# Chunks of v joined three steps ahead, and a fixed order of val, x and output on TensorE in the last batch

## The chip, the cores and the metric

One Trainium2 chip, one core of it. The metric is the device time of one execution in microseconds (us); lower is better. The engines are TensorE (PE), VectorE (DVE), ScalarE (ACT), GpSimd (POOL) and SyncE (SP), which here only issues DMAs.

## The reference

Four batches of 6336 rows and 256 channels. Per batch a channel attention: the scores are 256 x 256, and v is multiplied by the softmax `a`. Then a gated causal convolution over the rows.

```python
qn = q / (norm(q, axis=1) + 1e-06)          # over the 6336 rows; k alike
s = kn.transpose(0, 2, 1) @ qn / tau
a = softmax(s)                              # 256 x 256 for each batch
x = v @ a
gate = sigmoid(sum(conv_w[k] * xp[:, k:k + S] for k in range(5)))   # xp: x with 4 rows of zeros ahead
out = (gate * (x @ w_val)) @ w_out
```

## The kernel before

For each batch the kernel first works through groups of rows of q and k (scores and squares of norms), then a softmax, then the rows of v in 13 chunks of 508 rows (the last one 240). There are 52 such chunks, called steps here, numbered 0 to 51; the last batch's are 39 to 51. The scores of a batch are made between the steps of the batch before it, so steps 40 and later have no scores beside them.

The work of one step n, by function and line:

- v arrives with channels on partitions, as a high part `v_hi` and a remainder `v_lo` (TensorE multiplies the pairs in three products). Up to step 41 and for step 51 TensorE transposes it (`transpose_v`, L486). For steps 42 to 50 (`FROM = 42`) DMAs do it: `load_cols` (L454, a DMA transpose of 16-bit halves into `v_cols`), `spread_cols` (L463, four DMAs into `v_parts`, the split rows), and `join_parts` (L474): a copy of one half on ScalarE and of the other on GpSimd into `v_word` (L482), the cast to `v_hi` on ScalarE (L483), the subtraction to `v_lo` on GpSimd (L484).
- `conv` (L512): 12 matmuls into two banks `x_ps`, one for each half of the channels; for each half a first tap on ScalarE (L519) and four taps on VectorE (L523) into `gate`. There are two `x_ps` banks, so x of the next step needs the taps of this one done.
- `sigmoid` (L526) on ScalarE; `value` (L531): 12 matmuls into `val_ps`, and the product with the gate on VectorE (L541).
- `split_g` (L543): `g_hi` on ScalarE (L554), `g_lo` on GpSimd (L555). `finish` (L558): 24 matmuls (L574) with `w_out` into `o_ps`, two copies on ScalarE (L584), two stores that ScalarE issues (L589, L591).

The loop at L744 writes, for each n: the join of step n + 2, the transpose of n + 5 and the spread of n + 4, sigmoid(n), conv(n + 1), value(n), split_g(n), finish(n - 1). That is not yet the order of an engine: a scheduler with its own costs places the instructions, each engine then runs its list in order. `behind("NAME")` makes it place what stands inside behind the instruction noted under that name. Tiles come from pools: raw rows, `v_cols` from six slots "raw" of `raw_p`; split rows of q and k and `v_parts` from three slots "hi" of `split_p`; `v_hi` and `v_lo` from three slots each of `v_p`.

Of the kernel before, what the change touches and what calls it, by code (L numbers as in the profile page):

```python
# [9 lines left out]
F32R = mybir.dt.float32r  # L10
I32 = mybir.dt.int32
I64 = mybir.dt.int64
U16 = mybir.dt.uint16
# [5 lines left out]
P = 128  # L19
# [6 lines left out]
EARLY = 2  # L26
OWE = 3
FROM = 42
COLS_AHEAD = 5
PARTS_AHEAD = 4  # L30
HALO = 4
ROWS = 508

# [2 lines left out]
def kernel(  # L36
# [13 lines left out]
    nc = tc.nc  # L50
    B, N, C = q.shape
    K = conv_w.shape[0]
    NH = C // P
# [4 lines left out]
    raw_p = ctx.enter_context(tc.tile_pool(name="raw_p", bufs=6))  # L58
    split_p = ctx.enter_context(tc.tile_pool(name="split_p", bufs=3))
# [3 lines left out]
    v_p = ctx.enter_context(tc.tile_pool(name="v_p", bufs=VLEAD + 1))  # L63
# [46 lines left out]
    marks = {}  # L110
# [319 lines left out]
    WMAX = max(w for _, w in chunks)  # L430
    NT = -(-(HALO + WMAX) // P)

    vraw, vt = {}, {}
# [17 lines left out]
    SPAN = NT * P  # L451
    vcols, vparts = {}, {}

    def load_cols(b, i):  # L454

        t0, w = chunks[i]
        rows = -(-(HALO + w) // 16) * 16
        lo = min(t0 - HALO, N - rows)
        t = raw_p.tile([P, 2 * NH, SPAN], U16, name="v_cols", tag="raw")
        nc.sync.dma_start_transpose(out=t[:, :, 0:rows], in_=v[b, lo:lo + rows].bitcast(U16))  # L460
        vcols[b, i] = t, rows

    def spread_cols(b, i):  # L463

        t, rows = vcols.pop((b, i))
        d = split_p.tile([P, 2, NH, SPAN], U16, name="v_parts", tag="hi")
        half = P // 2
        for x in range(2):
            for s in range(2):
                nc.sync.dma_start(out=d[x * half:(x + 1) * half, s, :, 0:rows],  # L470
                                  in_=t[s:P:2, x:2 * NH:2, 0:rows])
        vparts[b, i] = d, rows

    def join_parts(b, i):  # L474

        d, rows = vparts.pop((b, i))
        n = HALO + chunks[i][1]
        vw = split_p.tile([P, NH, HALO + WMAX], F32, name="v_word", tag="sq")
        th, tl = vt[b, i] = [v_p.tile([P, NH, HALO + WMAX], F32R, name=name) for name in ("v_hi", "v_lo")]
        halves = vw.bitcast(U16).rearrange("p h (t s) -> p h s t", s=2)  # L480
        for h, copy in enumerate((nc.scalar.copy, nc.gpsimd.tensor_copy)):
            copy(halves[:, h, :, 0:n], d[:, :, h, rows - n:rows])  # L482
        marks["VH"] = nc.scalar.copy(th[:, :, 0:n], vw[:, :, 0:n])  # L483
        nc.gpsimd.tensor_tensor(tl[:, :, 0:n], vw[:, :, 0:n], th[:, :, 0:n].bitcast(F32), ALU.subtract)  # L484
# [46 lines left out]
    def value(b, i):  # L531
        w = chunks[i][1]
        gate = gates[b, i]
        vals = {}
        for halves in ((0,), (1,)) if (b, i) == all_steps[0] else ((0, 1),):
            for h in range(NH):
                if h not in vals:
                    vals[h] = ps.tile([P, 512], F32, name="val_ps", tag="bank")
                product(vals[h][:, 0:w], weights[b], 1, b, i, h, HALO, HALO + w, halves)
                if 1 in halves:  # L540
                    nc.vector.tensor_tensor(gate[:, h, 0:w], vals[h][:, 0:w], gate[:, h, 0:w], ALU.mult)  # L541
# [16 lines left out]
    def finish(b, i):  # L558
        t0, w = chunks[i]
        gh, gl = gts.pop((b, i))  # L560
        nt = -(-w // P)
        offs = [min(j * P, w - P) for j in range(nt)]
        o_sb = w_p.tile([P, NT, C], F32, name="o_sb")
        for j in range(0, nt, 2):
            pair = offs[j:j + 2]
            last = (b, i) == all_steps[-1]
            o_ps = ps.tile([P, 512], F32, name="o_ps", tag="bank")
            halves = [o_ps, ps.tile([P, 512], F32, name="o_ps", tag="bank") if last and len(pair) > 1 else o_ps]
            for u, off in enumerate(pair):
                n_ = 0  # L570
                o_ps = halves[u]
                for h in range(NH):
                    for gs, ws in ((gh, wo_hi), (gh, wo_lo), (gl, wo_hi)):
                        nc.tensor.matmul(o_ps[:, u * C:(u + 1) * C], gs[:, h, off:off + P], ws[:, h, :],  # L574
                                         start=n_ == 0, stop=n_ == 3 * NH - 1)
                        n_ += 1
            if (b, i) == all_steps[-1]:

                for u, (copy, dma) in enumerate(((nc.scalar.copy, nc.scalar), (nc.vector.tensor_copy, nc.sync))[:len(pair)]):
                    copy(o_sb[:, j + u, :], halves[u][:, u * C:(u + 1) * C])  # L580
                    first = max((j + u) * P - pair[u], 0)
                    dma.dma_start(out=out[b, t0 + pair[u] + first:t0 + pair[u] + P], in_=o_sb[first:P, j + u, :])
                continue
            marks["ACT"] = nc.scalar.copy(o_sb[:, j:j + len(pair), :], o_ps[:, 0:len(pair) * C].rearrange("p (j c) -> p j c", c=C))  # L584
        if (b, i) == all_steps[-1]:
            return
        full = w // P
        store = nc.sync if (b, i) == all_steps[-2] else nc.scalar
        store.dma_start(out=out[b, t0:t0 + full * P].rearrange("(j p) c -> p j c", p=P), in_=o_sb[:, 0:full, :])  # L589
        if w % P:  # L590
            store.dma_start(out=out[b, t0 + full * P:t0 + w], in_=o_sb[P - w % P:P, full, :])  # L591
# [3 lines left out]
    all_steps = [(b, i) for b in range(B) for i in range(NC)]  # L595
    by_dma = set(all_steps[FROM:-1])
# [6 lines left out]
    @contextmanager  # L603
    def behind(*engines):
        with ExitStack() as st:
            for e in engines:
                st.enter_context(tc.issue_after(marks[e].ins))
            yield
# [28 lines left out]
    def tick():  # L637
        if stages:
            with tc.high_priority():
                if next(stages[0], 0) is not None:  # L640
                    stages.pop(0)

    def step(n):
        return all_steps[n] if 0 <= n < len(all_steps) else None
# [76 lines left out]
    def end(n):  # L721

        return tc.high_priority() if n == len(all_steps) else nullcontext()
# [20 lines left out]
    for n in range(len(all_steps)):  # L744
        now, after, prev, new = step(n), step(n + 1), step(n - 1), step(n + VLEAD)
        if step(n + VLEAD + 1) and step(n + VLEAD + 1) not in by_dma:
            load_v(*step(n + VLEAD + 1))
        if new in by_dma:
            with behind("GH", "GL", "TAP"):
                join_parts(*new)  # L750
        if step(n + COLS_AHEAD) in by_dma:
            load_cols(*step(n + COLS_AHEAD))
        if step(n + PARTS_AHEAD) in by_dma:
            spread_cols(*step(n + PARTS_AHEAD))
        turns = due_after(n) - (issued - len(ready))
        for turn in range(turns):
            if turn == 0:
                run_group()
                if n == 0:
                    sigmoid(*now)  # L760
                with behind(*(["ACT", "VH"] + ["SIG"] * (n > 0) if n < EARLY else ["ACT", "GH"])):
                    split_group()
        tick()
        if n:
            with end(n + 1):
                sigmoid(*now)
        while after and after[0] not in weights:
            tick()
        if after:
            with end(n + 2):  # L770
                for h in range(NH):
                    conv(*after, h)
                marks["CONV"] = marks["PRODUCT"]
        tick()
        while now[0] not in whole:
            tick()
        with end(n + 1):
            value(*now)
        tick()
        turning = bool(stages)  # L780
        if not turning:
            with end(n + 1), behind("TAP0"):
                split_g(*now)
        for turn in range(turns):
            if turn == 1:
                run_group()
                with behind(*(["TAP", "GH"] if n < EARLY else ["ACT"])):
                    split_group()
        if new and new not in by_dma:
            with behind("AT"):  # L790
                for h in range(NH):
                    transpose_v(*new, h)
        tick()
        if turning:
            with behind("TAP0", "ATC"):
                split_g(*now)
        if prev:
            with behind(*{len(all_steps) - 2: ["CONV"], len(all_steps) - 1: ["G"]}.get(n, [])):
                finish(*prev)
    finish(*all_steps[-1])  # L800


# [30 lines left out]
```

## Time and profile before

| what | value |
|---|---|
| median of 3 runs | 642.15 us (641.31 to 642.46) |
| the profiled execution | 642.54 us, its span 640.8 us |
| busiest engines | PE 628.7 us, DVE 510.0 us, ACT 479.9 us, POOL 424.1 us |
| matmuls | 3975 |

The span reaches from the first to the last instruction on the chip. In the rows of a timeline the columns are start and duration in us, engine, line, operation, output and inputs, shape, count, and in brackets how long the engine stood idle ahead of it and what ended that. A waits row gives the waiting line, the one waited for, total us, times and the longest. In a table by stage each engine has its busy time with the number of instructions behind it; PEclk is the granted clock of TensorE.

### The profile page before, as it was taken

How to read it: one execution, taken by the hardware profiler on the slowest of the kernel's cores; microseconds unless marked ns; L12 is line 12 of the kernel's file. 1: busy time of each engine (PE TensorE's matmuls, PEld its weight loads, DVE VectorE, ACT ScalarE, POOL GpSimd, SP SyncE). 2: the span in 40 equal slices, each digit the busy share in tenths (PEclk: the TensorE clock that was granted, in tenths of full speed). 3: DMA queues.
4: the chain of work that ended last, by engine and by line, in shares of the span. 5: the costliest groups of instructions: out<-in, count | busy, mean ns of one | idle time of the engine just before them, and what ended most of it. 6: DMA issues, size and time to landing. Idle time of an engine off the chain costs nothing.

```text
span 640.8 us, 10757 instructions
## 1 busy us (share of the span) xinstructions
PE 628.7 (98%) x3975; PEld 564.4 (88%) x3975; DVE 510.0 (80%) x808; ACT 479.9 (75%) x620; POOL 424.1 (66%) x223
## 2 busy tenths in 40 slices
PE   8999999999999999999999999999999999998996
PEld 7898899999999989989998989999998898887885
DVE  4989897878788788868788779787878888867884
ACT  4877887868897696777788688778688566776754
POOL 1894699759555598768765669686675225586741
PEclk9999999999999999999999999999999999999999
DMA  8999665555533646546544556555689522442212
GB/s 264 399 374 340 216 214 172 179 183 164 162 110 126 220 161 212 188 136 194 156 151 132 172 163 211 187 170 139 157 187 196 152 83 86 125 129 76 66 60 87
DMA packets 93114, 110.48 MB, mean 172 GB/s; under 512 B 23484, under 2 KB 75142, under 8 KB 93062
## 3 DMA queue, kind: packets, MB, share of 16 engines
q1 hardware_dynamic: 67286, 84.48, 42.7%
q10 hardware_dynamic: 25776, 25.32, 12.7%
q8 instruction: 31, 0.51, 0.3%
q14 instruction: 21, 0.17, 0.1%
HBM read 74.39 MB, written 25.95 MB: 157 GB/s over the span
## 4 chain that ended last, share of the span: by engine, by line
PE 83%; ACT 5%; DVE 4%; POOL 3%; DMA 2%; issue 2%; SPq 1%; ACTq 0%; POOLq 0%
PE s_ps L322 23%; PE o_ps L574 19%; PE x_ps L505 18%; PE val_ps L505 17%; PE t_ps L495 5%; DVE gate L523 3%; PE o_ps L419 1%; POOL g_lo L555 1%; DMA raw<-in_k_dram 1%; POOL v_lo L484 1%; ACT gate L529 1%; DMA v_parts<-v_cols 1%; ACT o_sb L584 1%; SPq L88 0%; ACT gate L519 0%
## 5 line engine op out<-in xcount | busy, mean ns | idle before, releaser
L523 DVE SCALAR_TENSOR_TENSOR gate<-x_ps,cw,gate 128x508 f32<-128x508 f32 (+1 forms) x416 | 279.4, 718 | 19.7 <-ACT gate L519 17.0
L275 POOL TENSOR_TENSOR hi<-raw,hi 128x1536 fp32r<-128x1536 f32 (+3 forms) x62 | 180.5, 2916 | 66.1 <-ACT hi L274 64.2
L555 POOL TENSOR_TENSOR g_lo<-gate,g_hi 128x1016 fp32r<-128x1016 f32 (+1 forms) x50 | 116.4, 2327 | 65.3 <-ACT g_hi L554 60.0
L298 DVE TENSOR_TENSOR acc_ps<-acc_ps,sq 128x512 f32<-128x512 f32 (+1 forms) x135 | 94.1, 697 | 68.5 <-ACT sq L293 66.1
L505 PE MATMUL x_ps<-v_hi,w 128*128 128x512 f32 (+1 forms) x416 | 140.9, 393 | 1.9 <-DVE gate L523 1.8
L505 PE MATMUL val_ps<-v_hi,w 128*128 128x508 f32 (+1 forms) x416 | 133.9, 383 | 0.0
L322 PE MATMUL s_ps<-hi 128*128 128x256 f32 (+1 forms) x912 | 131.6, 289 | 0.2 <-ACT hi L274 0.2
L322 PEld LDWEIGHTS s_ps<-hi 128*128 128x128 f32 (+1 forms) x912 | 118.2, 190 | 4.6 <-POOL hi L275 0.8
L584 ACT COPY o_sb<-o_ps 128x512 f32<-128x512 f32 x99 | 58.1, 588 | 81.1 <-PE o_ps L574 80.8
L574 PE MATMUL o_ps<-wo_hi,g_lo 128*128 128x256 f32 x400 | 111.2, 282 | 2.1 <-POOL g_lo L555 2.1
L574 PE MATMUL o_ps<-wo_hi,g_hi 128*128 128x256 f32 x400 | 112.8, 283 | 0.0
L574 PE MATMUL o_ps<-wo_lo,g_hi 128*128 128x256 f32 x400 | 111.8, 281 | 0.0
L293 ACT ACTIVATE sq<-raw 128x1536 f32<-128x1536 f32 (+2 forms) x72 | 95.9, 1341 | 1.9 <-DMA raw<-in_k_dram 1.8
L505 PEld LDWEIGHTS x_ps<-v_hi,w 128*128 128x128 f32 x416 | 77.4, 188 | 17.8 <-issue 3.4
L519 ACT ACTIVATE gate<-x_ps,cw 128x508 f32<-128x508 f32 (+1 forms) x104 | 69.1, 671 | 30.1 <-PE x_ps L505 26.9
L505 PEld LDWEIGHTS val_ps<-v_hi,w 128*128 128x128 f32 x416 | 77.2, 188 | 14.5 <-ACT o_sb L584 0.4
L298 POOL TENSOR_TENSOR acc<-acc,sq 128x512 f32<-128x512 f32 x57 | 74.7, 1311 | 21.8 <-ACT sq L293 21.6
L541 DVE TENSOR_TENSOR gate<-val_ps,gate 128x508 f32<-128x508 f32 (+1 forms) x104 | 64.1, 657 | 26.1 <-ACT gate L529 26.1
L274 ACT CAST hi<-raw 128x1536 fp32r<-128x1536 f32 (+3 forms) x62 | 76.8, 1242 | 5.6 <-DMA raw<-in_k_dram 3.1
L505 PE MATMUL x_ps<-v_lo,w 128*128 128x512 f32 (+1 forms) x208 | 79.7, 383 | 0.0
L505 PE MATMUL val_ps<-v_lo,w 128*128 128x508 f32 (+1 forms) x208 | 79.1, 380 | 0.0
L574 PEld LDWEIGHTS o_ps<-wo_hi,g_lo 128*128 128x128 f32 x400 | 74.8, 189 | 2.9 <-POOL g_lo L555 2.7
(118 smaller groups left out, 807.6 us busy)
## 6 DMA issues: line engine op xcount, KB each, us to landing
raw<-in_q_dram SPq DMA_DIRECT2D x59, 384.0 KB
raw<-in_k_dram SPq DMA_DIRECT2D x59, 384.0 KB
out_dram<-o_sb ACTq DMA_DIRECT2D x47, 384.0 KB
v_raw<-in_v_dram SPq DMA_DIRECT2D x35, 512.0 KB
out_dram<-o_sb ACTq DMA_DIRECT2D x47, 124.0 KB
v_parts<-v_cols SPq DMA_DIRECT2D x36, 128.0 KB
raw<-in_q_dram SPq DMA_DIRECT2D x9, 256.0 KB
raw<-in_k_dram SPq DMA_DIRECT2D x9, 256.0 KB
```

What stands on the lines that cost most here:

```text
L274: cast = nc.scalar.copy(hi[r, js, :, 0, :], rows_of[r, js])
L275: nc.gpsimd.tensor_tensor(hi[r, js, :, 1, :], rows_of[r, js], hi[r, js, :, 0, :].bitcast(F32), ALU.subtract)
L293: nc.scalar.activation(sq[0:np_, ja:jb], rows_of[0:np_, ja:jb], AF.Square)
L298: add = eng.tensor_tensor(st[key][0:np_], st[key][0:np_], sq[0:np_, j], ALU.add)
L322: marks["SCORES"] = nc.tensor.matmul(st["s"][:, h, :], lhs, rhs, start=False, stop=stop and h == NH - 1 and n_ == len(ops) - 1)
L505: marks["PRODUCT"] = nc.tensor.matmul(ps, wt[:, which, ws, ch, hs], vs[:, ch, lo:hi_], start=ws == 0 and ch == 0 and vs is th, stop=ws == ...
L519: marks["TAP"] = nc.scalar.activation(gate[:, h, 0:w], x_ps[:, 0:w], AF.Copy, scale=cw[:, h:h + 1])
L523: marks["GATE"] = nc.vector.scalar_tensor_tensor(gate[:, h, 0:w], x_ps[:, tap:tap + w], cw[:, tap * NH + h:tap * NH + h + 1], gate[:, h, 0 ...
L541: nc.vector.tensor_tensor(gate[:, h, 0:w], vals[h][:, 0:w], gate[:, h, 0:w], ALU.mult)
L555: marks["GL"] = nc.gpsimd.tensor_tensor(gl[:, :, 0:w], gate[:, :, 0:w], gh[:, :, 0:w].bitcast(F32), ALU.subtract)
L574: nc.tensor.matmul(o_ps[:, u * C:(u + 1) * C], gs[:, h, off:off + P], ws[:, h, :], start=n_ == 0, stop=n_ == 3 * NH - 1)
L584: marks["ACT"] = nc.scalar.copy(o_sb[:, j:j + len(pair), :], o_ps[:, 0:len(pair) * C].rearrange("p (j c) -> p j c", c=C))
```

## The change

1. A chunk is joined three steps ahead instead of two (`JOIN_AHEAD`), and its transpose and spread are issued a step earlier each (6 and 5 ahead).
2. The split rows `v_parts` lie in the "raw" slots. The joined pair of an odd chunk of a batch lies in a "hi" slot as one tile `v_pair`, that of an even chunk in `v_p` as before.
3. In steps 40 to 49 (`steady`) the order on TensorE is fixed by `behind`: val(n) behind the output of the step before, x(n + 1) behind val(n), the output of n - 1 behind x(n + 1).

```diff
@@ -26,8 +26,9 @@
 EARLY = 2
 OWE = 3
 FROM = 42
-COLS_AHEAD = 5
-PARTS_AHEAD = 4
+JOIN_AHEAD = 3
+PARTS_AHEAD = 5
+COLS_AHEAD = 6
 HALO = 4
 ROWS = 508
 
@@ -463,7 +464,7 @@
     def spread_cols(b, i):
 
         t, rows = vcols.pop((b, i))
-        d = split_p.tile([P, 2, NH, SPAN], U16, name="v_parts", tag="hi")
+        d = raw_p.tile([P, 2, NH, SPAN], U16, name="v_parts", tag="raw")
         half = P // 2
         for x in range(2):
             for s in range(2):
@@ -476,7 +477,11 @@
         d, rows = vparts.pop((b, i))
         n = HALO + chunks[i][1]
         vw = split_p.tile([P, NH, HALO + WMAX], F32, name="v_word", tag="sq")
-        th, tl = vt[b, i] = [v_p.tile([P, NH, HALO + WMAX], F32R, name=name) for name in ("v_hi", "v_lo")]
+        if i % 2:
+            pair = split_p.tile([P, 2, NH, HALO + WMAX], F32R, name="v_pair", tag="hi")
+            th, tl = vt[b, i] = [pair[:, x] for x in range(2)]
+        else:
+            th, tl = vt[b, i] = [v_p.tile([P, NH, HALO + WMAX], F32R, name=name) for name in ("v_hi", "v_lo")]
         halves = vw.bitcast(U16).rearrange("p h (t s) -> p h s t", s=2)
         for h, copy in enumerate((nc.scalar.copy, nc.gpsimd.tensor_copy)):
             copy(halves[:, h, :, 0:n], d[:, :, h, rows - n:rows])
@@ -571,8 +576,8 @@
                 o_ps = halves[u]
                 for h in range(NH):
                     for gs, ws in ((gh, wo_hi), (gh, wo_lo), (gl, wo_hi)):
-                        nc.tensor.matmul(o_ps[:, u * C:(u + 1) * C], gs[:, h, off:off + P], ws[:, h, :],
-                                         start=n_ == 0, stop=n_ == 3 * NH - 1)
+                        marks["OUT"] = nc.tensor.matmul(o_ps[:, u * C:(u + 1) * C], gs[:, h, off:off + P], ws[:, h, :],
+                                                         start=n_ == 0, stop=n_ == 3 * NH - 1)
                         n_ += 1
             if (b, i) == all_steps[-1]:
 
@@ -745,9 +750,9 @@
         now, after, prev, new = step(n), step(n + 1), step(n - 1), step(n + VLEAD)
         if step(n + VLEAD + 1) and step(n + VLEAD + 1) not in by_dma:
             load_v(*step(n + VLEAD + 1))
-        if new in by_dma:
+        if step(n + JOIN_AHEAD) in by_dma:
             with behind("GH", "GL", "TAP"):
-                join_parts(*new)
+                join_parts(*step(n + JOIN_AHEAD))
         if step(n + COLS_AHEAD) in by_dma:
             load_cols(*step(n + COLS_AHEAD))
         if step(n + PARTS_AHEAD) in by_dma:
@@ -766,16 +771,21 @@
                 sigmoid(*now)
         while after and after[0] not in weights:
             tick()
+        steady = 40 <= n < len(all_steps) - 2
+        if steady:
+            with behind(*(["O"] if "O" in marks else [])):
+                value(*now)
         if after:
-            with end(n + 2):
+            with end(n + 2), behind(*(["PRODUCT"] if steady else [])):
                 for h in range(NH):
                     conv(*after, h)
                 marks["CONV"] = marks["PRODUCT"]
         tick()
         while now[0] not in whole:
             tick()
-        with end(n + 1):
-            value(*now)
+        if not steady:
+            with end(n + 1), behind(*(["O"] if "O" in marks else [])):
+                value(*now)
         tick()
         turning = bool(stages)
         if not turning:
@@ -795,8 +805,12 @@
             with behind("TAP0", "ATC"):
                 split_g(*now)
         if prev:
-            with behind(*{len(all_steps) - 2: ["CONV"], len(all_steps) - 1: ["G"]}.get(n, [])):
+            with behind(*{len(all_steps) - 2: ["CONV"], len(all_steps) - 1: ["G"]}.get(n, ["CONV"] if steady else [])):
                 finish(*prev)
+            if steady:
+                marks["O"] = marks["OUT"]
+            else:
+                marks.pop("O", None)
     finish(*all_steps[-1])
```

Lines of the kernel after are numbered a little higher: L510 is the product of before's L505, L579 L574, L524 and L534 the first tap and the sigmoid, L559 g_hi, L487 and L488 the copy and the cast of the join, L589 the output copy, L594 and L596 the stores, L461 and L471 the transpose and the spread.

TensorE before, from the end of val of step 45 on, with the output of step 44 behind it (step 45 has the same pattern one step later):

```order
L505 MATMUL val_ps<-v_lo,w 128x508
L505 MATMUL val_ps<-v_hi,w 128x508
L574 MATMUL o_ps<-wo_hi,g_hi 128x256
L574 MATMUL o_ps<-wo_lo,g_hi 128x256
L574 MATMUL o_ps<-wo_hi,g_hi 128x256
L574 MATMUL o_ps<-wo_lo,g_hi 128x256
L574 MATMUL o_ps<-wo_hi,g_lo 128x256
```

TensorE after, at the same place:

```order
L510 MATMUL val_ps<-v_hi,w 128x508 x2
L510 MATMUL val_ps<-v_lo,w 128x508
L510 MATMUL val_ps<-v_hi,w 128x508
L510 MATMUL x_ps<-v_pair,w 128x512 x12
L579 MATMUL o_ps<-wo_hi,g_hi 128x256
L579 MATMUL o_ps<-wo_lo,g_hi 128x256
L579 MATMUL o_ps<-wo_hi,g_lo 128x256
L579 MATMUL o_ps<-wo_hi,g_hi 128x256
```

Ahead of the output of step 44 now stand the twelve products x of step 46, whose chunk lies in `v_pair`; before, they stood behind that output.

ScalarE before, from the sigmoid of step 45 on:

```order
L529 ACTIVATE gate<-gate 128x1016
L589 DMA out_dram<-o_sb 128x3x256
L483 CAST v_hi<-v_word 128x1024
L591 DMA out_dram<-o_sb 124x256
L519 ACTIVATE gate<-x_ps,cw 128x508
L554 CAST g_hi<-gate 128x1016
L519 ACTIVATE gate<-x_ps,cw 128x508
L482 COPY v_word<-v_parts 128x2x512
L584 COPY o_sb<-o_ps 128x512
```

ScalarE after, from the same sigmoid on:

```order
L534 ACTIVATE gate<-gate 128x1016
L524 ACTIVATE gate<-x_ps,cw 128x508 x2
L559 CAST g_hi<-gate 128x1016
L487 COPY v_word<-v_parts 128x2x512
L488 CAST v_pair<-v_word 128x1024
L589 COPY o_sb<-o_ps 128x512 x2
L594 DMA out_dram<-o_sb 128x3x256
L596 DMA out_dram<-o_sb 124x256
L534 ACTIVATE gate<-gate 128x1016
```

Both first taps now follow the sigmoid directly, ahead of g_hi and of the join's copy and cast; the two output copies and the two stores stand together at the end, right ahead of the next sigmoid.

SyncE before, from the last two transposes (steps 49 and 50) to the last stores:

```order
L460 DMA_TRANSPOSE v_cols<-in_v_dram 128x4x512 x2
L446 DMA v_raw<-in_v_dram 128x4x256 x2
L446 DMA v_raw<-in_v_dram 128x256
L448 DMA v_raw<-in_v_dram 116x256
L470 DMA v_parts<-v_cols 64x2x512 x24
L589 DMA out_dram<-o_sb 128x3x256
```

SyncE after, from the last loads of v on:

```order
L447 DMA v_raw<-in_v_dram 128x256
L449 DMA v_raw<-in_v_dram 116x256
L471 DMA v_parts<-v_cols 64x2x512 x4
L461 DMA_TRANSPOSE v_cols<-in_v_dram 128x4x512
L471 DMA v_parts<-v_cols 64x2x512 x4
L461 DMA_TRANSPOSE v_cols<-in_v_dram 128x4x512
L471 DMA v_parts<-v_cols 64x2x512 x4
L461 DMA_TRANSPOSE v_cols<-in_v_dram 128x4x512
L471 DMA v_parts<-v_cols 64x2x512 x8
L594 DMA out_dram<-o_sb 128x3x256
```

The last three transposes (steps 48 to 50) now stand between the spreads of steps 46 to 49, each in the slot of a chunk that has been spread; before, all transposes were issued ahead of the last six spreads.

## The prediction

> **What bounds the kernel now.** I read the head of the page, then a table by stage, then TensorE's waits in the stage that changes.
>
> ```profile
> span 640.8 us, 10757 instructions
> PE 628.7 (98%) x3975; PEld 564.4 (88%) x3975; DVE 510.0 (80%) x808; ACT 479.9 (75%) x620; POOL 424.1 (66%) x223
> ...
> 500.00:535.21 35.21, 35.21 (x224) 31.56 (x222) 29.63 (x51) 21.17 (x33) 9.51 (x5) 1.00 0.29 91
> 535.21:620.58 85.37, 82.75 (x474) 71.61 (x472) 65.38 (x98) 60.76 (x78) 53.50 (x27) 1.00 0.34 94
> 620.58:640.80 20.22, 13.16 (x98) 12.00 (x96) 11.29 (x22) 8.01 (x16) 4.95 (x3) 0.94 0.29 90
> ```
>
> TensorE is busy 98% of the span, at full clock until the end, so a change can only win what TensorE loses in waits, or cut work; this one cuts no work. TensorE's order first differs from before at 535.21 us, behind val of step 40. The second stage reaches from there to the first matmul of val of step 50. What it should take follows from undisturbed groups in the chain that ended last:
>
> ```profile
> 519.29 2.77 PE x_ps L505 x12
> 522.05 2.83 PE o_ps L574 x24
> 524.88 2.73 PE val_ps L505 x12
> 527.61 0.87 PE t_ps L495 x8
> ```
>
> The stage holds ten outputs (steps 39 to 48), nine val (41 to 49), ten x (41 to 50) and four transposes: 28.3 + 24.6 + 27.7 + 0.4 = 81.0 us at these paces. It takes 85.4, so 4.4 us are lost. The busy column hides part of that (it shows 2.6 idle), because a matmul's recorded time runs on past its issue. A full step is 2.73 + 2.77 + 2.83 = 8.33 us. Who is waited for, first in total from 535 us on, then one by one:
>
> ```profile
> PE o_ps L574 <- POOL g_lo L555: 2.1, 3, 1.5
> PE x_ps L505 <- DVE gate L523: 1.6, 3, 0.6
> ...
> 587.58 0.28 PE L574 MATMUL o_ps<-wo_lo,g_hi 128*128 128x256 f32 x1
> 589.33 0.38 PE L574 MATMUL o_ps<-wo_hi,g_lo 128*128 128x256 f32 x1 [1.47 <-POOL g_lo L555]
> ...
> 552.77 0.28 PE L574 MATMUL o_ps<-wo_lo,g_hi 128*128 128x256 f32 x1
> 553.51 0.47 PE L505 MATMUL x_ps<-v_hi,w 128*128 128x512 f32 x1 [0.47 <-DVE gate L523]
> ...
> 624.09 0.35 PE L505 MATMUL x_ps<-v_hi,w 128*128 128x244 f32 x1 [0.62 <-DVE gate L523]
> ...
> 625.52 0.35 PE L505 MATMUL x_ps<-v_hi,w 128*128 128x244 f32 x1 [0.52 <-DVE gate L523]
> ```
>
> The output product waits for g_lo; x waits until VectorE's taps free its bank. No v_hi or v_lo of a join is in that list. Behind the largest wait stands this:
>
> ```profile
> 580.79 0.59 ACT L584 COPY o_sb<-o_ps 128x512 f32<-128x512 f32 x1 [2.16 <-PE o_ps L574]
> 581.98 0.59 ACT L584 COPY o_sb<-o_ps 128x512 f32<-128x512 f32 x1 [0.60 <-PE o_ps L574]
> 582.46 1.06 ACT L529 ACTIVATE gate<-gate 128x1016 f32<-128x1016 f32 x1
> 583.42 1.04 ACT L483 CAST v_hi<-v_word 128x1024 fp32r<-128x1024 f32 x1
> 584.36 0.68 ACT L519 ACTIVATE gate<-x_ps,cw 128x508 f32<-128x508 f32 x1
> 584.93 1.04 ACT L554 CAST g_hi<-gate 128x1016 fp32r<-128x1016 f32 x1
> ...
> 583.55 1.28 DVE L541 TENSOR_TENSOR gate<-val_ps,gate 128x508 f32<-128x508 f32 x2 [2.01 <-ACT gate L529]
> ...
> 584.53 2.42 POOL L484 TENSOR_TENSOR v_lo<-v_word,v_hi 128x1024 fp32r<-128x1024 f32 x1 [3.99 <-ACT v_hi L483]
> 586.90 2.37 POOL L555 TENSOR_TENSOR g_lo<-gate,g_hi 128x1016 fp32r<-128x1016 f32 x1
> ```
>
> The sigmoid of step 45 (582.46) stands on ScalarE behind copies that wait for TensorE; so the product with val ends at 584.83, g_hi at 585.97, and g_lo, itself behind v_lo on GpSimd, at 589.27. TensorE wanted the output of step 45 at 587.1, only 2.3 us after the product.
>
> **The change, part by part.**
>
> Joins three ahead. The same two copies, cast and subtraction, nine times, in the same place of a step but for a chunk one step later. Nothing waits for them on TensorE, so by themselves they are worth 0. The first join (chunk 42) falls ahead of 535 us, into the 8.42 us that GpSimd stands idle there (row below): 0. Their cost is room on GpSimd: a v_lo may stand before a g_lo, at 2.42 us, twice in a row at one place (the pair of steps 45 and 46).
>
> Slots. Split rows go where raw rows lay, odd joined chunks where split rows lay. No instruction is added. SyncE's order changes: transposes 48 to 50, issued before 500 us until now, come between the spreads. Prices:
>
> ```profile
> 522.08 1.23 POOL L555 TENSOR_TENSOR g_lo<-gate,g_hi 128x480 fp32r<-128x480 f32 x1 [3.88 <-PE x_ps L505]
> 531.73 2.41 POOL L555 TENSOR_TENSOR g_lo<-gate,g_hi 128x1016 fp32r<-128x1016 f32 x1 [8.42 <-ACT g_hi L554]
> ...
> 535.48 2.58 SPq L470 DMA_DIRECT2D v_parts<-v_cols  x4
> ...
> 582.51 3.61 DMA v_parts<-v_cols
> ...
> L460 SPq DMA_TRANSPOSE v_cols<-in_v_dram x9: 1851/3237/5046, 432.5 to 493.3; - x9
> ```
>
> A spread takes 2.6 us to issue and up to 3.6 to land; the transpose that takes over its slot waits for that landing and issues in 3.2. That makes some 9 us a step, against 8.33. The first of these spreads (46) waits for the slot that the join of chunk 42 empties: on GpSimd its copy now stands right behind the g_lo that ends at 523.3, so it ends at 524.7 (1.4 us, a copy's row is below). So the last transpose (50) is issued by 524.7 + 3 x 9.1 = 552, and by 555 to 557 it has landed. The stores of steps 39, 40 and 41 on ScalarE now wait for transposes 48, 49 and 50 (they share semaphores); the store of step 41 comes at about 560. Room of 3 us or more: 0, hidden by the two steps between.
>
> Order. In steps 40 to 49 TensorE now does val(n), x(n+1), output(n-1). I walk one step, t = 0 at val(n), with these rows beside those above:
>
> ```profile
> 529.97 0.69 ACT L519 ACTIVATE gate<-x_ps,cw 128x508 f32<-128x508 f32 x1 [0.81 <-PE x_ps L505]
> ...
> 531.49 0.69 ACT L519 ACTIVATE gate<-x_ps,cw 128x508 f32<-128x508 f32 x1
> ...
> 530.69 5.66 DVE L523 SCALAR_TENSOR_TENSOR gate<-x_ps,cw,gate 128x508 f32<-128x508 f32 x8
> ...
> 565.42 5.32 DVE L523 SCALAR_TENSOR_TENSOR gate<-x_ps,cw,gate 128x508 f32<-128x508 f32 x8
> ...
> 566.54 1.37 ACT L482 COPY v_word<-v_parts 128x1024 uint16<-128x1024 uint16 x1
> ```
>
> x(n+1)'s halves are complete at 2.73 + 1.39 + 0.2 = 4.3 and 5.7 (0.2: a matmul's record past its issue). ScalarE's first taps end at 5.0 and 6.4. VectorE's eight taps in the new order take turns between the halves, so they run 5.32 from 5.7, to 11.05. ScalarE meanwhile does, from 6.3: the cast v_hi (0.95), g_hi(n) (0.95), a copy for the join (1.25), two output copies (1.1), the issue of two stores (0.8): 11.3. (Steps without a wait count from start to start, about 0.1 less than the rows: 583.42 to 584.36.) Sigmoid(n+1) 11.3 to 12.4, product with val(n+1) to 13.7. The second half's tap of the next step is ready at 8.33 + 6.4 = 14.7, and VectorE needs 0.7 before it: 0.3 us of room, and x's banks are free at 10.4 and 11.05 where x(n+2) wants them at 11.06 and 12.4. So the loop over VectorE and ScalarE just fits under TensorE's 8.33. The output of step n+1 comes at 2 x 8.33 + 5.5 = 22.2, 8.5 us after its product instead of 2.3; g_hi (16.4 to 17.4 at the latest) and g_lo (2.4) end near 20, or 22 behind a double v_lo. So the waits for g_lo go, and the output copies, which held up the sigmoid, no longer wait just before it.
>
> Terms. (1) The 4.4 us of the stage go: -4.4. (2) One new wait: x(41) now stands at 535.21, but the taps of step 40, in alternating order, run 530.7 and then from 532.2, when the second half's first tap is ready: the first half is done near 536.2, so x(41) starts at 536.3: +1.1. Queued behind it are output(39) and all after. (3) The seams: each group now starts behind a wait on another engine; a row of the trace gives about 0.1 where a group starts afresh (0.47 against 0.39 us in the record of x at 553.51), so 0 to 10 x 0.1; I take +0.1, since most operands are there long before. (4) The end. x(50) starts at 536.3 + 9 x 8.33 + 0.4 = 611.7, its first tap can run at 613.3 instead of 619.0. VectorE is free at 614.4: product 49 ends 13.7 - 8.3 = 5.4 us into its step, which starts at 608.6, and half of v_lo(51) is 0.4:
>
> ```profile
> 619.00 0.69 ACT L519 ACTIVATE gate<-x_ps,cw 128x508 f32<-128x508 f32 x1 [1.33 <-PE x_ps L505]
> ...
> 614.89 0.72 DVE L497 TENSOR_TENSOR v_lo<-t_ps,v_hi 128x244 fp32r<-128x244 f32 x2
> 619.72 5.66 DVE L523 SCALAR_TENSOR_TENSOR gate<-x_ps,cw,gate 128x508 f32<-128x508 f32 x8 [2.34 <-ACT gate L519]
> ...
> 630.61 4.28 PE o_ps L574 x36
> ```
>
> So its eight taps end at 620.1, and x(51), due at 617.4 + 2.7 = 620.1 and 620.8, finds its banks free: the two waits of 0.62 and 0.52 go: -1.1. Behind that TensorE has output 49, val(51) and 4.28 us of last outputs, without a wait now as before. Sum: -4.4 + 1.1 + 0.1 - 1.1 = -4.3 us. The profiled execution took 642.54 (span 640.8 and 1.7 around it): 638.2. The median of the runs shown is 642.15, 0.4 lower: 637.8.
>
> Term 2 rests on TensorE not passing a waiting matmul: at 552.77 the next row is the waiting x itself, and nothing ran in those 0.47 us although outputs stood behind. The Trainium skill ("TensorE: Matmul & The Clock Gate", Measured speedup vs the span model) says that matmuls start and end in program order without reordering. This trace agrees; by the rule the 1.1 us are paid in full, and could output(39) pass x(41), the sum would be -5.4.
>
> **The rivals.**
>
> A. The loop over ScalarE and VectorE sets the pace. Its room is 0.3 us, and every ScalarE operation between tap and sigmoid counts. With the sigmoid 0.55 us later than walked, a step is 0.25 longer, over nine steps +2.2; half of the gain goes: 640.0. For it: the sigmoid was late in this trace at nearly every step (VectorE's wait of 2.01 above). Against: those waits came from copies behind late outputs, which the new order takes out. If all of the gain goes, it is no change, 642.
>
> B. Slower: no tap overlaps anything. In the old order two steps had the product with val between taps; in the new one it is always taps, sigmoid, product. If VectorE goes on waiting 2.01 us for the sigmoid as in the row above, the loop is 0.7 + 5.32 + 2.01 + 1.28 = 9.3. It decides from 8.33 + 4.3 / 9 = 8.8 a step, and 9.3 costs 9 x 0.5: 4.5 above the median, 646.6. For it: the steps take 8.9 on average now ((619.0 - 530.0) / 10, by first taps). Against: with x ahead of the output the second half is ready while VectorE still does the product, and the copy that made up most of the 2.01 is gone.
>
> C. The store waits. If spreads and transposes land as late as the longest issue row (5.05) each time, the last transpose is 3 x 1.8 = 5.4 us later, at 562, and the store of step 41 holds ScalarE by 2.4, less the room of 0.3: +2.1, so 639.9.
>
> D. The g_lo waits stay at the double v_lo: one wait of 0.5 to 1.5, within the range.
>
> **How the numbers follow.** Forecast (gain 3.0 to 5.4): 0.66. A or C with half the gain (1.3 to 3.0): 0.18. Nothing left, within 0.2%, which is about what a measurement of this kernel can tell: 0.09. B, slower: 0.07. The forecast's own range is 636.7 to 639.2. To leave out 2 in 10 the range goes up through A and C to 640.6 and down to the sum without terms 2 and 3, 636.6. Faster by over 0.2%: 0.84; same 0.09; slower 0.07.
>
> **What would show it.** Right: from 535 to the end no wait of the output for g_lo; first taps of steps 41 to 50 at even distances of 8.3 to 8.4; one wait of about 1 us of x for VectorE near 535; val(50) at 617.4; v_lo on GpSimd no longer waiting long for v_hi at the expense of g_lo. Wrong: distances of 8.7 or more with VectorE waiting for the sigmoid at each step (A, B); a store issue on ScalarE that ends with a transpose's landing (C). The prediction fails if the loop of VectorE and ScalarE needs more than 8.33.

## The result, and the profile after

| | median us | runs | ratio to before (95%) |
|---|---|---|---|
| before | 642.31 | 4 (641.31 to 642.79) | |
| changed | 637.38 | 4 (636.75 to 637.62) | 0.9924 (0.9907 to 0.9941) |

The change wins 4.9 us; 637.8 was forecast. The profiled execution took 637.19 us. The head of its page, and the table by stage with the stages cut at the same places of the program (where val of step 40 has ended, and where val of step 50 starts):

```profile
span 635.4 us, 10771 instructions
PE 625.7 (98%) x3975; PEld 563.4 (89%) x3975; DVE 507.1 (80%) x808; ACT 479.9 (76%) x620; POOL 424.5 (67%) x223
...
534.77:617.19 82.42, 81.48 (x474) 71.66 (x474) 65.85 (x101) 59.62 (x76) 51.54 (x26) 1.00 0.35 99
617.19:635.40 18.21, 12.72 (x98) 12.01 (x96) 9.32 (x20) 7.20 (x14) 3.16 (x3) 0.91 0.33 100
```

The second stage took 85.37 us and takes 82.42, the end took 20.22 and takes 18.21. Another 0.44 us (the stage starts at 534.77 instead of 535.21) lie ahead of both, where the program on TensorE is the same: the first tap of step 40, at 529.97 before and 529.48 in the row below, stood anywhere from 528.3 to 530.9 in the twelve traces of this study. So kernels are compared below also by the time from that row to the end of the span, which this scatter does not touch: 110.8 before, 105.9 after.

TensorE's waits from 530 us to the end, of which there is one, and then the chain that ended last (start, us, engine, tile, line, count):

```profile
PE x_ps L510 <- DVE gate L528: 0.9, 1, 0.9
```

```profile
531.71 4.03 DVE gate L528 x6
...
535.87 3.01 PE x_ps L510 x12
538.88 2.83 PE o_ps L579 x24
541.71 2.73 PE val_ps L510 x12
544.44 2.81 PE x_ps L510 x12
...
620.11 1.36 PE x_ps L510 x12
621.47 2.83 PE o_ps L579 x24
624.30 1.34 PE val_ps L510 x12
625.64 4.28 PE o_ps L579 x36
```

All three waits for g_lo are gone, and so are the three of x for VectorE's taps, two of which lay at the end; one wait of x(41) for those taps has come. Behind it the chain is TensorE alone for 94 us, in the order x, output, val. One of these steps on the other engines:

```profile
529.48 0.69 ACT L524 ACTIVATE gate<-x_ps,cw 128x508 f32<-128x508 f32 x1 [0.28 <-PE x_ps L510]
...
561.33 1.05 ACT L534 ACTIVATE gate<-gate 128x1016 f32<-128x1016 f32 x1 [0.90 <-DVE gate L528]
562.68 0.69 ACT L524 ACTIVATE gate<-x_ps,cw 128x508 f32<-128x508 f32 x1 [0.29 <-PE x_ps L510]
564.01 0.69 ACT L524 ACTIVATE gate<-x_ps,cw 128x508 f32<-128x508 f32 x1 [0.65 <-PE x_ps L510]
564.59 1.04 ACT L488 CAST v_pair<-v_word 128x1024 fp32r<-128x1024 f32 x1
565.53 1.04 ACT L559 CAST g_hi<-gate 128x1016 fp32r<-128x1016 f32 x1
566.47 1.38 ACT L487 COPY v_word<-v_parts 128x1024 uint16<-128x1024 uint16 x1
567.72 1.06 ACT L589 COPY o_sb<-o_ps 128x512 f32<-128x512 f32 x2
568.81 0.38 ACTq L594 DMA_DIRECT2D out_dram<-o_sb  x1
569.23 0.40 ACTq L596 DMA_DIRECT2D out_dram<-o_sb  x1
569.68 1.06 ACT L534 ACTIVATE gate<-gate 128x1016 f32<-128x1016 f32 x1 [0.90 <-DVE gate L528]
...
604.46 0.69 ACT L524 ACTIVATE gate<-x_ps,cw 128x508 f32<-128x508 f32 x1 [0.57 <-PE x_ps L510]
...
562.42 1.28 DVE L546 TENSOR_TENSOR gate<-val_ps,gate 128x508 f32<-128x508 f32 x2 [1.36 <-ACT gate L534]
563.62 0.74 DVE L528 SCALAR_TENSOR_TENSOR gate<-x_ps,cw,gate 128x508 f32<-128x508 f32 x1
564.73 4.67 DVE L528 SCALAR_TENSOR_TENSOR gate<-x_ps,cw,gate 128x508 f32<-128x508 f32 x7 [0.37 <-ACT gate L524]
```

ScalarE waits for x at both first taps, so TensorE sets the pace: five steps from 562.68 to 604.46 are 8.36 each. The sigmoid's 0.90 of idle time is a trap of reading: nearly all of it is the issue of the two stores (568.81 to 569.63), which is not counted as busy. ScalarE's own spare time in a step is 0.29 + 0.65, and it reaches the sigmoid 0.3 us behind VectorE's last tap (564.73 + 4.67 = 569.40).

### The profile page after: what moved, and what is told of

Read it like the earlier page. It is cut to its first block, busy times and chain, and to the rows that moved or that the text cites. A ratio compares the mean times of both kernels' runs of the same rounds, so it can differ in the third digit from the quotient of the medians.

```text
span 635.4 us, 10771 instructions
## 1 busy us (share of the span) xinstructions
PE 625.7 (98%) x3975; PEld 563.4 (89%) x3975; DVE 507.1 (80%) x808; ACT 479.9 (76%) x620; POOL 424.5 (67%) x223
## 4 chain that ended last, share of the span: by engine, by line
PE 93%; ACT 3%; DMA 1%; DVE 1%; issue 1%; SPq 0%; ACTq 0%
PE s_ps L323 23%; PE o_ps L579 21%; PE x_ps L510 21%; PE val_ps L510 20%; PE t_ps L500 5%; PE o_ps L420 1%; DMA raw<-in_k_dram 1%; DVE gate L528 1%; SPq L89 0%; ACT g_hi L559 0%; ACT L389 0%; ACT o_sb L589 0%; ACT v_hi L501 0%; PE o_ps L356 0%; ACT gate L524 0%
## 5 line engine op out<-in xcount | busy, mean ns | idle before, releaser
L510 PE MATMUL x_ps<-v_hi,w 128*128 128x512 f32 (+1 forms) x376 | 126.1, 392 | 1.2 <-DVE gate L528 1.2
L510 PE MATMUL val_ps<-v_hi,w 128*128 128x508 f32 (+1 forms) x376 | 120.2, 382 | 0.0
L579 PE MATMUL o_ps<-wo_hi,g_hi 128*128 128x256 f32 x400 | 112.9, 283 | 0.0
L579 PE MATMUL o_ps<-wo_lo,g_hi 128*128 128x256 f32 x400 | 112.1, 281 | 0.0
L579 PE MATMUL o_ps<-wo_hi,g_lo 128*128 128x256 f32 x400 | 111.6, 281 | 0.0
L589 ACT COPY o_sb<-o_ps 128x512 f32<-128x512 f32 x99 | 57.3, 587 | 67.0 <-PE o_ps L579 65.6
L524 ACT ACTIVATE gate<-x_ps,cw 128x508 f32<-128x508 f32 (+1 forms) x104 | 68.9, 669 | 29.8 <-PE x_ps L510 29.1
L510 PEld LDWEIGHTS x_ps<-v_hi,w 128*128 128x128 f32 x376 | 69.9, 188 | 14.9 <-issue 2.0
L510 PEld LDWEIGHTS val_ps<-v_hi,w 128*128 128x128 f32 x376 | 69.7, 188 | 12.4
L579 PEld LDWEIGHTS o_ps<-wo_hi,g_hi 128*128 128x128 f32 x400 | 75.6, 189 | 0.9
L579 PEld LDWEIGHTS o_ps<-wo_lo,g_hi 128*128 128x128 f32 x400 | 75.6, 189 | 0.6
L579 PEld LDWEIGHTS o_ps<-wo_hi,g_lo 128*128 128x128 f32 x400 | 75.1, 189 | 0.0
```

Of the source, the lines that this page charges most:

```text
L510: marks["PRODUCT"] = nc.tensor.matmul(ps, wt[:, which, ws, ch, hs], vs[:, ch, lo:hi_], start=ws == 0 and ch == 0 and vs is th, stop=ws == ...
L524: marks["TAP"] = nc.scalar.activation(gate[:, h, 0:w], x_ps[:, 0:w], AF.Copy, scale=cw[:, h:h + 1])
L579: marks["OUT"] = nc.tensor.matmul(o_ps[:, u * C:(u + 1) * C], gs[:, h, off:off + P], ws[:, h, :], start=n_ == 0, stop=n_ == 3 * NH - 1)
```

## The experiments

All were timed against the kernel before, on the same chip as it; the table draws on three chips. "From tap 40" is the time from the first tap of step 40 to the end of the span, in the one profiled execution of each; the two kernels that were profiled twice agree within 0.1 us by it.

| kernel | median us | ratio to before (95%) | from tap 40 |
|---|---|---|---|
| before | 642.0 to 642.6 | | 110.8 |
| changed (again) | 637.42 | 0.9921 (0.9908 to 0.9935) | 105.9 (106.0) |
| order alone | 640.01 | 0.9958 (0.9944 to 0.9972) | 108.4 |
| order and slots, joins two ahead | 640.83 | 0.9981 (0.9972 to 0.9990) | 109.4 |
| joins and slots, no fixed order | 639.22 | 0.9947 (0.9935 to 0.9960) | 107.7 |
| order val, output, x | 652.92 | 1.0161 (1.0147 to 1.0176) | 121.5 |
| order alone, g_lo behind v_lo | 649.41 | 1.0112 (1.0098 to 1.0126) | 117.4 |
| two more copies a step on ScalarE | 637.64 | 0.9932 (0.9918 to 0.9945) | 106.4 |
| four more copies a step | 639.38 | 0.9956 (0.9942 to 0.9969) | 108.5 |
| output begun ahead of x (again) | 637.19 (636.68) | 0.9920 (0.9907 to 0.9932), 0.9910 (0.9897 to 0.9923) | 105.1 (105.2) |

**The order alone.** The changed kernel with before's lead and slots:

```diff
-JOIN_AHEAD = 3
-PARTS_AHEAD = 5
-COLS_AHEAD = 6
+JOIN_AHEAD = 2
+PARTS_AHEAD = 4
+COLS_AHEAD = 5
...
-        d = raw_p.tile([P, 2, NH, SPAN], U16, name="v_parts", tag="raw")
+        d = split_p.tile([P, 2, NH, SPAN], U16, name="v_parts", tag="hi")
...
-        if i % 2:
+        if False:
```

> The fixed order alone: joins two ahead and all slots as before. Theory (the order on TensorE carries the gain, the joins by themselves are worth 0): TensorE has exactly the changed kernel's order, so 637.2 to 638.0. What differs is ScalarE's order: in five of the steps the cast of a join stands ahead of the first tap and g_hi between the two taps; the loop there is 1.05 + 0.95 + 0.69 + 0.95 + 0.69 + six taps of 0.67 = 8.35, just TensorE's 8.33, so at most +0.5. Rival (the joins carry a part, because v_lo of a chunk comes too late for x, which now stands ahead of the output): waits of x for v_lo on TensorE and 639 or more.

It wins 2.6 us, only half of the change. TensorE's waits, and GpSimd and TensorE at the first of them:

```profile
PE x_ps L510 <- POOL v_lo L489: 3.5, 2, 1.7
...
548.68 2.41 POOL L560 TENSOR_TENSOR g_lo<-gate,g_hi 128x1016 fp32r<-128x1016 f32 x1 [3.07 <-ACT g_hi L559]
551.04 1.35 POOL L487 COPY v_word<-v_parts 128x1024 uint16<-128x1024 uint16 x1
552.33 2.36 POOL L489 TENSOR_TENSOR v_lo<-v_word,v_hi 128x1024 fp32r<-128x1024 f32 x1
554.89 2.40 POOL L489 TENSOR_TENSOR v_lo<-v_word,v_hi 128x1024 fp32r<-128x1024 f32 x1 [0.21 <-ACT v_hi L488]
...
554.74 0.50 PE L510 MATMUL x_ps<-v_lo,w 128*128 128x512 f32 x1 [1.73 <-POOL v_lo L489]
```

The rival of the expectation holds. Where GpSimd does two v_lo in a row, the first of them stands behind a g_lo and the next chunk's copy, and ends at 554.69; x wanted it at 552.8. In the order of before x came 2.8 us later, behind the output, and had time.

The list has no wait of x(41), though x(41) stands ahead of the output here too. At step 40 VectorE's second tap (531.99) goes on with the first half, and the first half is done in time; in the changed kernel the second tap (531.71) belongs to the second half, for which VectorE idles 0.30 us, and the first half is done only at 535.73. So the fixed order by itself does not bring the wait of about 1 us; it takes the alternating taps as well, which came with the earlier joins. This is read from the lists; no run changed the tap order by itself.

**The slots or the lead?** The changed kernel with one number changed, `JOIN_AHEAD = 2`.

> The fixed order, the new slots, transposes and spreads as early as in the changed kernel, but the joins two steps ahead as before. Every engine but SyncE has the order of the run with the order alone. Theory (the third step of lead is what keeps v_lo from coming late where GpSimd does two v_lo in a row): the same two waits of x for v_lo, 3.5 us together, and 639.5 to 640.5. Rival (the old slots held the spreads and with them the joins up): no such wait, 637.4.

```profile
PE x_ps L510 <- POOL v_lo L489: 3.4, 2, 1.7
```

The same two waits. The time, 640.83, is 0.3 us above the expected range. Of the 1.0 us from tap 40 beyond the run before, half lies behind the last copy on VectorE, where no engine computes any more (6.03 us to the end of the span, 5.53 there); the cause stays open. So the new slots and the earlier transposes by themselves win nothing here; the third step of lead ends the two waits, and is what the new order needs.

**The joins alone.** The changed kernel with `steady = False`.

> Joins three ahead and the new slots, without the fixed order. Theory as recorded (the joins by themselves are worth 0): 642.3, as before. Rival: with the earlier joins the scheduler writes another order by itself: val, half of x, 23 matmuls of the output, the other half of x, the last of the output, at every step from 42 on; first taps of the first half are done before the sigmoid, the loop is 0.69 + 1.05 + 0.55 + 0.95 + 0.95 + 0.69 + four taps of 0.67 = 7.6, and the output comes 5 us after its product: no g_lo wait of over 0.5, and x(41) comes behind the output, so no wait of 1.1 there: 636.5 to 638.

```profile
PE o_ps L579 <- POOL g_lo L560: 1.0, 1, 1.0
PE x_ps L510 <- DVE gate L528: 0.9, 1, 0.9
...
571.63 1.39 PE x_ps L510 x6
573.02 2.70 PE o_ps L579 x23
575.72 1.37 PE x_ps L510 x6
577.09 0.12 PE o_ps L579
```

This contradicts the recorded theory: 3.1 us are won (107.7 against 110.8 from tap 40) without the fixed order. The scheduler, given the earlier joins, writes val, half of x, 23 matmuls of the output, the other half of x, one of the output, at every step from 43 to 48 (the last four rows show one). With half of x ahead of it the output comes late enough: g_lo of step 43 ends at 572.68, and its output is the second of these rows. The two waits above and 0.4 us at the end remain. The rival's mechanism is right; its time was 1.2 us low, and it had allowed no wait for g_lo of over 0.5. Earlier joins under exactly the old order of TensorE were not run, so that the new order carries this gain is read from the trace and not shown by a run.

**Any fixed order?** Val, output, x in steps 40 to 49:

```diff
+            if steady:
+                with behind("PRODUCT"):
+                    finish(*prev)
-            with end(n + 2), behind(*(["PRODUCT"] if steady else [])):
+            with end(n + 2), behind(*(["OUT"] if steady else [])):
                 for h in range(NH):
                     conv(*after, h)
...
```

The rest of the edit leaves out the `finish` further down in these steps and places val(n) behind x(n).

> A fixed order too, but val, output, x in steps 40 to 49; joins as in the changed kernel. Theory (what counts is whether ScalarE's and VectorE's loop fits under 8.33 us): the output's copies, the stores' issue and the cast now stand between sigmoid and taps: 1.05 + 0.55 + 0.42 + 0.95 + 0.42 + 0.69 + 0.95 + 0.69 + six taps of 0.67 = 9.7 a step, so nine steps lose up to 1.3 each: 645 to 648, slower than before, with x waiting for VectorE's taps. Rival (any regular order does it, since it ends the waits for g_lo): 637 to 638.5. Second rival: the output comes only 2.9 us after its product, so g_lo is waited for about 0.7 each step, 9 x 0.7 = 6: 643.

```profile
PE o_ps L579 <- POOL g_lo L560: 9.7, 8, 1.3
PE x_ps L510 <- DVE gate L528: 2.2, 1, 2.2
...
573.16 0.38 PE L579 MATMUL o_ps<-wo_hi,g_lo 128*128 128x256 f32 x1 [1.21 <-POOL g_lo L560]
```

Slower than before by 10 us, and slower than any of the three expectations. A step takes 9.8 to 10.0 us from output to output, where 9.7 was foreseen, but the loss does not show where the theory put it: TensorE waits for g_lo at eight outputs, as the second rival said, though 1.2 us each and not 0.7, and only once for taps. Both are one loop: the output waits for g_lo, x stands behind the output, and the taps, sigmoid, product and g_lo of the next step stand behind x. The changed kernel differs in the place of x, ahead of the output, and has neither the loop nor its waits.

**No double v_lo with two ahead?** The order alone, with g_hi and g_lo of steps 41 to 48 behind the v_lo of the join:

```diff
-            with end(n + 1), behind("TAP0"):
+            with end(n + 1), behind("TAP0", *(["VL"] if 41 <= n <= 48 else [])):
                 split_g(*now)
...
```

> The order alone with joins two ahead, and g_hi and g_lo of steps 41 to 48 placed behind the v_lo of the join, so that GpSimd never does two v_lo in a row. Theory (with two ahead GpSimd has no order that serves both): v_lo is in time, but g_lo, now always behind v_lo, ends 0.5 us or so after TensorE wants it: 9 x 0.6, about 642 with the waits of the output for g_lo, none for v_lo. Rival (only the double v_lo was at fault): no waits on either, 637 to 637.5.

```profile
PE x_ps L510 <- POOL v_lo L489: 6.0, 8, 0.8
PE x_ps L510 <- DVE gate L528: 2.9, 6, 0.5
...
ACT gate L524 <- POOL g_lo L560: 20.3, 8, 2.7
```

A miss: 649.4, and not by waits for g_lo on TensorE. The last row, ScalarE's waits, shows what the expectation had left out: the first tap writes a `gate` tile, of which there are two, and waits 2.5 us for the g_lo that still reads it. The cast of the join stays a step behind its copy, so v_lo is late as well, at eight steps instead of two. That GpSimd has no order that serves both with two ahead was expected from a walk and is not shown by this run; it shows only that this order is worse.

**How much room has ScalarE?** The changed kernel with copies that feed nothing, two a step (and four, with `range(4)`), behind the second half's first tap:

```diff
+        elif 41 <= all_steps.index((b, i)) <= 49:
+            with behind("TAP"):
+                for _ in range(2):
+                    marks["TAP"] = nc.scalar.copy(junk, zeros.bitcast(F32))
...
```

> The changed kernel with two more copies of 128x512 on ScalarE in each of steps 41 to 49, behind the second half's first tap; they feed nothing. About 1.0 us a step. By the recorded walk (0.3 us of room in the loop of ScalarE and VectorE): 9 x 0.7 = 6.3 more, 643.5. By the trace of the changed kernel (ScalarE stands idle 0.90 us ahead of the sigmoid and 0.29 + 0.65 ahead of the taps of each step): nothing, 637.2 to 637.8.

> The same with four copies, about 2.0 us a step. By the recorded walk 9 x 1.7 = 15 more: 652. By the idle time of ScalarE in the changed kernel, 1.84 a step: 9 x (2.0 - 1.84) = 1.4 and a little for the start, 638.5 to 641; x then waits for VectorE's taps at every step.

```profile
571.93 1.05 ACT L539 ACTIVATE gate<-gate 128x1016 f32<-128x1016 f32 x1 [0.90 <-ACT o_sb L594]
572.89 1.42 ACT L525 ACTIVATE gate<-x_ps,cw 128x508 f32<-128x508 f32 x2
574.20 0.61 ACT L531 COPY junk<-zeros 128x512 f32<-128x512 f32 x1
```

With two (rows above: ScalarE goes without a pause from the sigmoid into the taps) 18 copies of 0.51 us, 9.2 us of work, cost 0.4 to 0.5 us from tap 40. The walk's 6.3 is refuted; the room is about 1 us a step, the spare time ahead of the two taps. The walk had charged the delay of the sigmoid anew in every step. Here the sigmoids start at 562.56, 571.93, 580.32 and 588.81: one distance of 9.4, then 8.4 and 8.5.

With four copies TensorE waits four times for taps, the first time for x(41), where the expectation had a wait at every step, and ScalarE's sigmoids follow one another at 8.7 us:

```profile
PE x_ps L510 <- DVE gate L533: 2.3, 4, 0.9
```

18.4 us of work cost 2.5. The time lies in the expected range, but for a wrong reason: the 0.90 counted as idle was the issue of the stores. Part of that issue now runs beside copies (last section), which gives some room instead; how much was not measured by itself.

**The wait of x(41).** The changed kernel with `FIRST = {40: 10, 41: 6, 42: 2}` matmuls of the output placed ahead of x:

```diff
+        outs, ahead = prev and outputs(*prev), FIRST.get(n, 0)
+        if ahead:
+            with behind("PRODUCT"):
+                for _ in range(ahead):
+                    next(outs)
         if after:
-            with end(n + 2), behind(*(["PRODUCT"] if steady else [])):
+            with end(n + 2), behind(*((["OUT"] if ahead else ["PRODUCT"]) if steady else [])):
...
```

Here `outputs` is `finish` with a `yield` behind each matmul, and the rest of it runs where `finish` ran.

> The changed kernel, but 10, 6 and 2 matmuls of the output go ahead of x in steps 40, 41 and 42. Theory (x(41) waits 1.1 us because the taps of step 40 are late only there, and the loop has 0.3 to 0.4 us of room a step to catch up): x(41) starts without a wait and x(42) to x(44) come 0.2 to 0.5 earlier than 8.33 after one another: 636.1 to 636.6. Rival (the loop has no such room, it is paced at 8.33): the wait moves on to x(42) and x(43), 637.2.

> The changed kernel as it is, beside the next on one chip: 637.4, with one wait of about 1.0 us of x(41) for VectorE's taps in its profile.

> The same kernel as in the run with 10, 6 and 2 matmuls of the output ahead of x. Theory (the wait of 1.1 us is gone for good): 0.8 to 1.1 us below the changed kernel beside it, so 636.4 where that is at 637.4. Rival (the wait comes back elsewhere): the same time within 0.3.

In both profiles the list of TensorE's waits from 520 us to the end is empty, and x(41) starts right behind the tenth matmul of the output:

```profile
536.35 0.28 PE L584 MATMUL o_ps<-wo_hi,g_hi 128*128 128x256 f32 x1
536.47 0.40 PE L511 MATMUL x_ps<-v_hi,w 128*128 128x512 f32 x1
```

From tap 40 it takes 105.1 and 105.2 against 105.9 and 106.0, so 0.8 us less, the low end of what was expected. The medians (637.19, where 636.1 to 636.6 was expected; then 636.68 beside 637.42) do not settle it: the intervals overlap, so by the time of a whole execution this version is not shown to be faster than the changed one. It is the shortest of all from tap 40, and in that stretch the profile lists no wait of TensorE.

## Why the prediction was right, and where not

- **Term 1, the stage's 4.4 us go.** Right. From start to start between matmuls, the stage now loses 0.2 us beside the new wait.
- **Term 2, x(41) waits 1.1.** Right: 0.94 in the record, 1.10 from start to start. The output of step 39 stood behind it and did not pass, though its g_lo had ended at 533.58 and x(41) started only at 535.87. The Trainium skill says that matmuls stay in program order ("TensorE: Matmul & The Clock Gate", The mechanism, right ahead of the section that the prediction names). This trace agrees, and taking the wait away by order won 0.8 of the 1.1.
- **Term 3, seams 0.1.** Nothing found: but for x(41), the first matmul of each group of the stage follows the one ahead of it at the usual distance. Terms 1 to 3 together: -3.2 said, -2.95 measured (85.37 to 82.42).
- **Term 4, the end, -1.1.** Right in kind, too small: from val(50) to the last copy on VectorE it is 14.34 (620.58 to 634.92) against 12.75 (617.19 to 629.94), so -1.6. The two waits had been taken at their records, 0.62 and 0.52; from start to start they were 0.78 and 0.68, and the matmul behind each came 0.07 late too. For the profiled execution 638.2 was said and 637.19 came, 1.0 less: 0.5 from this term, 0.4 between the last copy and the end of the span, with no cause that these runs show, and 0.4 ahead of the stage, which is scatter; Terms 1 to 3 take 0.25 of it back.
- **Joins worth 0 by themselves.** The step that failed, though the sum did not feel it. From tap 40, joins earlier, without the order, win 3.1 us, as the scheduler then writes another order; the order without them wins 2.4, because v_lo comes late twice. "Nothing waits for them on TensorE" was read off an order in which x stands 2.8 us later; it had to be asked again for the new one. The walk of the new order never asks when v_lo is ready for x. That it was in time three steps ahead is in part luck, and the sum, which priced both parts together, came out right without having said why. The two gains do not add: each ends most of the same waits.
- **The loop's room of 0.3 us (rivals A and B).** Much too small for ScalarE: about 1 us more a step cost 0.4 to 0.5 in all. The walk had let every ScalarE operation push the next tap; in fact both first taps wait for x, 0.29 and 0.65 us in the rows above. The times that it gave for a step were good: it put the sigmoid 11.3 us behind the start of val of the step before, and from val of step 42 (549.93) to the sigmoid of step 43 (561.33) it is 11.4.
- **The lag of 8.5 us from product to output.** Right: the product of step 42 ends at 555.3, and its output starts at 563.8. At the double v_lo (chunks 45 and 46, rival D) g_lo of step 43 runs from 568.09 to 570.49 and ends 1.7 us ahead of its output, so rival D did not come.
- **SyncE and the stores (rival C).** The last transpose is issued at 549.99, said by 552, and the store of step 41 at 560.46 follows its copy, which ends at 560.44, without a wait:

```profile
549.99 2.07 SPq L461 DMA_TRANSPOSE v_cols<-in_v_dram  x1
...
560.46 0.38 ACTq L594 DMA_DIRECT2D out_dram<-o_sb  x1
```

## What to carry to other kernels

Before a part of a change is priced at nothing because nothing waits for it, ask for whom it comes later or earlier in the order that the rest of the change makes: here TensorE waited for no join in the old order, and in the new one the lead is worth 3.5 us from tap 40 (2.5 against the run that has the old slots as well). Where one engine is 98% busy, lay out one period for each engine, and look for the work whose operand is made last: put work whose operands have long been there ahead of it, as x went ahead of the output here, and then ask whether those operands still come in time in the new place. Time alone would not have told these parts apart; counting from a common instruction took out the scatter of what comes ahead of it, 2.6 us between the earliest and the latest of these traces.

## What the runs showed of the hardware

A wait costs TensorE more than its record: records of 0.94, 1.73 and 1.21 us were 1.10, 1.91 and 1.37 from start to start. A matmul is recorded past the point where the next one can start: those of val stand 0.23 us apart in the changed kernel, with records of 0.39. And the matmul behind the one that waited comes another 0.07 to 0.11 late.

In these traces ScalarE issues a store beside a copy of its own, when the copy stands ahead of the issue in its list and the store does not need it. In the kernel with four more copies:

```profile
569.07 0.68 ACT L531 COPY junk<-zeros 128x512 f32<-128x512 f32 x1
569.26 0.38 ACTq L599 DMA_DIRECT2D out_dram<-o_sb  x1
569.68 0.40 ACTq L601 DMA_DIRECT2D out_dram<-o_sb  x1
570.12 0.62 ACT L531 COPY junk<-zeros 128x512 f32<-128x512 f32 x1 [0.38 <-ACT junk L531]
```

The first issue runs while the copy does; the next copy starts at 570.12, behind the end of the second issue at 570.08. In the changed kernel no such copy stands there, and the two issues, 0.82 us from first to last, make up nearly all of the 0.90 us that ScalarE stands idle ahead of the sigmoid. The Trainium skill says that the recorded time of such a DMA instruction is spent on the sequencer, and that moving the data is not in it ("Perfetto Trace Analysis", DMA Instruction — HWDGE (DVE, Sync)). The rows above agree with the first half: the copy goes on through the 0.38 us of the first issue.
